# Index read and weight loads in one run on GpSimd, flag read last, contiguous w1 columns, and a new order of the work in an attention + mixture-of-experts kernel

## Chip, cores and metric

One NeuronCore of one Trainium2 chip. The metric is the device time of one execution in microseconds (us). All operands are float32. TensorE is called PE in the rows (PEld is its weight load), VectorE DVE, ScalarE ACT, GpSimd POOL, SyncE SP.

## What is computed

Two attention blocks with 32 inducing points, then a mixture of experts with one expert for each row. Cut to what matters:

```python
B, N, m, C = 4, 11456, 32, 128           # x: [B, N, C]; inducing: [m, C]; E, F = 8, 1024
def mab(q, kv):
    s = scale * (q @ kv.T); s = s - s.max(-1)
    a = exp(s); a /= a.sum(-1) + 1e-9
    return a @ kv
h = mab(inducing, x)                      # [B, 32, C]: needs all of x of its batch
x2 = mab(x, h)                            # [B, N, C]
logits = x2 @ w_gate;  e_idx = argmax(logits)        # one expert for a row
gate_w = softmax(logits)[e_idx];  eom = sigmoid(x2 @ w_output_gate)
out = gate_w * eom[e_idx] * (relu(x2 @ w1[e_idx]) @ w2[e_idx])
```

## The kernel before

The fast path guesses that all rows of a batch choose the same expert (that of the mean of h) and that the signs inside the relu are the same for all rows; then the expert's output is a linear map of the attention weights, and its values can be worked out once for the 32 points (`V`, 32 x 128) instead of for each row. `known` proves the guess at the end and leaves a flag for each batch; where a flag is set, a branch ("general") redoes that batch. It isn't taken here.

A batch is 90 tiles of 128 rows in six chunks: chunk 0 with 10 tiles, five with 16 (1 MB each). For every batch the kernel runs these steps (generators; each `yield Step(...)` names the engine, a planned cost, what it waits for and which ring slots it takes or gives back):

- `bring_in(b, k)`: load a chunk of x on SP's DMA queue into one of 5 chunk buffers (ring `c`, L109), transpose its tiles on PE (L226), copy them from PSUM to `xT` on ACT or DVE (L298). Chunk 0 and the first two full chunks of batch 0 come in two pieces.
- `attend_in(b, i)`: for one or two chunks the scores on PE (L254), max on DVE (L259), exp on ACT (L277), transpose on DVE (L281), and p times x on PE (L291), after which the chunk buffers are given back.
- `finish(b)`: merge the groups to h (`hs`, PE L325/L327, DVE L330 to L343).
- `choose(b)`: PE L352 multiplies the mean of h with the gate weights, DVE takes the index of the largest (L355, L358, tile `ix`), GpSimd reads it into a register (`value_load`, L361) and issues the DMAs of that expert's w1 and w2 (512 KB each, L369 and L374).
- `gates(b)`: small operations on GpSimd or DVE (L380 to L396) and two small matmuls (L399, L415) that make the gate matrix `gb`.
- `values(b)`: PE L426 multiplies h with w1 (four column groups of 256), DVE transposes and masks (L429 to L435), PE L444 multiplies with w2, L452 sums over the four groups, and a copy leaves `vb`, that is V(b).
- `weigh(b, k)`: scores of a chunk against h (PE L520), max (DVE L525, L528), exp (ACT L530).
- `attend_out(b, i)`: for two chunks the gate logits (PE L545) and a chain of small operations (`gate`, L610 to L635) that ends in the scale `sm`; then the output matmuls with `vb` (PE L563) and the scaling of four pieces of each chunk (`scaled`: L586 on DVE, L580 on ACT followed by L582 on GpSimd, L589 on ACT), and the stores on SP's queue (L598).

No loop runs over these steps. `interleave` is a planner that runs when the program is built: it keeps a clock for every engine, and takes at each turn the step that can start first, with a key from the table `ORDER` to decide between steps of the same start. The order in which it takes them is the order of the instructions on each engine; each engine works its queue strictly in that order. SP has one queue for the loads of x and the stores of out, so a load behind a store waits for that store's data. Its model has constants: `LAG` (from the end of a step to who waits for it), `COLD` (until 9 us a step on PE counts double), and fillers: matmuls of the identity that keep PE busy (`fill`, L154), put in wherever the plan has PE idle before `WARM`.

```python
LAG = {"T": 0.2, "V": 0.12, "A": 0.14, "G": 0.15, "D": 2.0, "S": 0.1}
...
if e == "T" and free[e] < WARM:
    fill(int((start - free[e]) / FILL), rings["bank"][-1][1])
```

At the end of the program every engine loads the flag from `flags` (L818) and branches (L819). The two DVE instructions that fill `flags` (L816, L817) and the load are written behind the planned part, where the compiler orders them.

Of the kernel before, what the change touches and what calls it, by code (L numbers as in the profile page):

```python
# [20 lines left out]
EPS = 1e-9
CH = 16
G = 4
# [5 lines left out]
        -362.6, -249.4, -297.0, -141.1, -66.2, -225.8, -56.5, -44.3, -26.1, 0.9, -18.1, -291.1,  # L29
        -91.2, -232.5, -91.6, -90.0, -72.7, -148.2, -142.0, -114.3, -68.9, -12.2, -87.6, 12.3,  # L30
    ],
    "attend_in": [
        -232.4, -227.2, -218.8, -345.7, -218.6, -218.3, -212.8, -232.0, -214.5, -164.2, -143.6, -218.7,
        -147.0, 3.8, -105.9, -148.6,
    ],
    "weigh": [
        -375.2, -216.8, 45.8, -90.0, -326.3, 62.3, -92.7, -171.9, -232.0, -150.7, -162.5, -102.5,
        -19.7, -114.3, -267.8, -92.2, -216.8, -284.7, -213.9, 144.4, -279.9, -332.7, -65.4, -332.0,
    ],
    "attend_out": [-109.6, -67.0, 12.7, -37.8, -310.4, 159.8, 2.0, -51.7, 11.5, -47.5, -1.7, -104.8],  # L40
    "finish": [-0.2, -80.8, -47.5, -116.3],
    "choose": [-80.8, -265.7, -279.2, -368.1],
    "gates": [41.2, -16.3, -2.9, -149.0],
    "values": [-71.8, 12.2, -60.8, -217.9],
    "known": [-85.5],
# [15 lines left out]
def body(ctx: ExitStack, tc: tile.TileContext, x, inducing, w_gate, w_out_gate, w1, w2, out):  # L61
# [93 lines left out]

    def interleave(threads):
        free = dict.fromkeys(LAG, 0.0)
        done = {}
# [689 lines left out]
```

## Time and profile before

| what | value |
|---|---|
| time, three runs | 208.21 us median (207.98, 208.21, 209.38) |
| the profiled execution | 209.38 us; its span, first to last instruction, 207.7 us |
| granted TensorE clock, mean | 0.946 |
| DMA | 51.75 MB, 249 GB/s over the span |

Starts and durations in rows are us from the span's start. [...] The profiled execution is the slowest of the three runs, 0.56% over their median.

### The profile page before, as it was taken

To read this page: it belongs to the slowest core of one execution; us is meant where nothing else is said; L and a number is where in the kernel's file an instruction comes from. 1 tells how busy PE (TensorE), PEld (TensorE's weight loads), DVE (VectorE), ACT (ScalarE), POOL (GpSimd) and SP (SyncE) were. 2 spreads that over 40 slices of the span, in tenths; PEclk is the share of its full clock that TensorE was granted. 3 is DMA by queue.
4 is the path that set the end of the run, shared out by engine and by line. 5 is a ranking of instruction groups with operands and counts; after the bars stand their busy time and mean duration, and the time that the engine had idled before them with its cause. 6 is when DMAs were issued, how large, how long until landed. Compare 5 with 4: busy or idle time off the path is not lost.

```text
span 207.7 us, 6550 instructions
## 1 busy us (share of the span) xinstructions
PE 175.7 (85%) x2627; PEld 123.8 (60%) x2628; DVE 138.7 (67%) x408; ACT 116.0 (56%) x299; POOL 48.1 (23%) x98
## 2 busy tenths in 40 slices
PE   6999998799799899997699999839999958895700
PEld 6987675775583675767268684627587523564700
DVE  2033863557569689894278889738968894999920
ACT  2268285453663755757057564904958882697400
POOL 1000000005001054330012612402325480535510
PEclk9999999999999999999699999979999996999665
DMA  5991765596419308999910999943337999479892
GB/s 180 353 400 21 271 249 196 215 360 264 190 21 372 140 3 248 374 383 385 419 66 14 323 386 396 357 155 126 97 107 307 379 338 349 177 228 371 292 345 108
DMA packets 12675, 51.75 MB, mean 249 GB/s; under 512 B 1760, under 2 KB 1792, under 8 KB 10336
## 3 DMA queue, kind: packets, MB, share of 16 engines
q1 hardware_dynamic: 11152, 47.06, 60.2%
q0 software_dynamic: 1152, 4.19, 5.8%
q8 instruction: 22, 0.36, 0.7%
q14 instruction: 13, 0.11, 0.1%
q10 hardware_dynamic: 336, 0.02, 0.1%
HBM read 27.81 MB, written 23.46 MB: 247 GB/s over the span
## 4 chain that ended last, share of the span: by engine, by line
PE 54%; DMA 19%; DVE 13%; issue 5%; POOL 3%; ACT 1%; POOLq 1%; DVEq 0%
PE bank L226 13%; DMA w1t<-in_moe_w_dram 10%; PE bank L291 9%; PE bank L254 8%; PE bank L563 8%; DMA c<-in_x_dram 6%; DVE ob L586 5%; PE bank L545 4%; PE bank L154 3%; DMA w2t<-in_moe_w_dram 3%; PE bank L520 2%; PE bank L426 2%; PE bank L327 1%; PE bank L444 1%; DVE am L525 1%
## 5 line engine op out<-in xcount | busy, mean ns | idle before, releaser
L298 ACT COPY xT<-bank 128x512 f32<-128x512 f32 (+1 forms) x74 | 39.0, 585 | 26.2 <-PE bank L226 26.0
L226 PEld LDWEIGHTS bank<-ident,c 128*128 128x128 f32 x360 | 39.6, 143 | 15.1 <-issue 6.7
L226 PE MATMUL bank<-ident,c 128*128 128x128 f32 x360 | 45.6, 276 | 3.5 <-DMA c<-in_x_dram 3.2
L582 POOL TENSOR_TENSOR ob<-ob,sm 128x512 f32<-128x512 f32 (+1 forms) x24 | 24.6, 1026 | 36.7 <-ACT ob L580 32.2
L563 PEld LDWEIGHTS bank<-vb,pT 32*128 32x128 f32 x720 | 25.8, 200 | 9.5 <-issue 5.2
L563 PE MATMUL bank<-vb,pT 32*128 32x128 f32 x720 | 30.3, 298 | 1.1 <-DVE lt L610 0.6
L586 DVE TENSOR_TENSOR ob<-bank,sm 128x512 f32<-128x512 f32 (+2 forms) x47 | 29.2, 647 | 2.1 <-PE bank L563 1.6
L580 ACT COPY ob<-bank 128x512 f32<-128x512 f32 (+1 forms) x24 | 13.7, 569 | 24.6 <-issue 10.3
L589 ACT ACTIVATE ob<-bank,sm 128x128 f32<-128x128 f32 x91 | 26.1, 394 | 0.0
L254 PE MATMUL bank<-xT,indT 128*32 128x512 f32 (+1 forms) x192 | 25.1, 591 | 0.4 <-DVE nb L271 0.4
L520 PE MATMUL bank<-xT,hc 128*32 128x512 f32 (+1 forms) x192 | 23.6, 598 | 0.1
L291 PE MATMUL bank<-c,p 128*32 128x128 f32 x720 | 22.8, 274 | 0.2 <-DVE p L281 0.2
L530 ACT ACTIVATE pT<-bank,nq 128x512 f32<-128x512 f32 (+1 forms) x24 | 16.1, 681 | 11.1 <-DVE nq L528 7.4
L259 DVE TENSOR_REDUCE cm<-bank 128x1 f32<-128x512 f32 (+1 forms) x24 | 15.4, 647 | 9.7 <-PE bank L254 9.6
L291 PEld LDWEIGHTS bank<-c,p 128*32 128x32 f32 x720 | 19.9, 110 | 3.3 <-issue 1.2
L298 DVE COPY xT<-bank 128x512 f32<-128x512 f32 (+1 forms) x18 | 12.1, 672 | 14.6 <-PE bank L226 14.6
L277 ACT ACTIVATE bank<-bank,nb 128x512 f32<-128x512 f32 (+1 forms) x24 | 15.5, 647 | 2.2 <-DVE nb L271 2.0
L281 DVE STREAM_TRANSPOSE p<-bank 128x512 f32<-128x512 f32 (+1 forms) x24 | 16.0, 668 | 0.9 <-ACT bank L277 0.8
L525 DVE TENSOR_REDUCE am<-bank 128x1 f32<-128x512 f32 (+1 forms) x24 | 15.2, 642 | 0.7 <-PE bank L520 0.5
L615 POOL TENSOR_SCALAR s<-lt 128x32 f32<-128x32 f32 (+1 forms) x12 | 3.8, 321 | 46.2 <-DVE lt L610 29.9
L545 PE MATMUL bank<-pT,gb 128*32 128x256 f32 (+1 forms) x192 | 12.8, 384 | 0.0
L426 PE MATMUL bank<-w1t,hs 128*32 128x256 f32 x32 | 4.5, 639 | 9.5 <-DMA w1t<-in_moe_w_dram 9.5
(121 smaller groups left out, 177.5 us busy)
## 6 DMA issues: line engine op xcount, KB each, us to landing
c<-in_x_dram SPq DMA_DIRECT2D x18, 1024.0 KB, 8.2
out_dram<-ob SPq DMA_DIRECT2D x30, 512.0 KB, 5.1
out_dram<-ob SPq DMA_DIRECT2D x8, 448.0 KB, 4.1
c<-in_x_dram SPq DMA_DIRECT2D x4, 512.0 KB, 11.0
w1t<-in_moe_w_dram POOLq DMA_DIRECT2D x4, 512.0 KB, 6.2
w2t<-in_moe_w_dram POOLq DMA_DIRECT2D x4, 512.0 KB, 7.1
out_dram<-ob SPq DMA_DIRECT2D x8, 256.0 KB, 4.6
c<-in_x_dram SPq DMA_DIRECT2D x3, 640.0 KB, 10.7
```

What stands on the lines that cost most here:

```text
L226: nc.tensor.transpose(t[:, j - a * G, :], xc[:, j, :], ident)
L254: nc.tensor.matmul(sj[r, 0:n, :], indT, xT[:, 0:n, r], start=True, stop=True)
L291: nc.tensor.matmul(h[r, :], p1[:, j, q, :], xc[:, q, :], start=j == 0 and q < G, stop=j == J - 1 and q >= n - G)
L298: (nc.scalar.copy if e == "A" else nc.vector.tensor_copy)(dst, src)
L520: nc.tensor.matmul(s[g * M : (g + 1) * M, :], st["hc", b], xT[:, q0[g] : q0[g] + w, :], start=True, stop=True)
L525: nc.vector.tensor_reduce(am, s, AX.X, ALU.max, apply_absolute_value=True)
L530: nc.scalar.activation(pT[:, base : base + w, :].rearrange("p a t -> p (a t)"), s, AF.Exp, bias=nq)
L545: nc.tensor.matmul(L[r, u, :], lhs, pT[:, 0:S, r], start=True, stop=True)
L563: nc.tensor.matmul(y[g][:, a, :], pT[r, t + a, :], st["vb", b][r, :], start=True, stop=True)
L582: nc.gpsimd.tensor_tensor(out=o, in0=o, in1=scale_by, op=ALU.mult)
L586: nc.vector.tensor_tensor(out=o, in0=y, in1=scale_by, op=ALU.mult)
L589: nc.scalar.activation(o[:, a, :], y[:, a, :], AF.Copy, scale=sv[:, a : a + 1])
```

## The change

- `choose`: one step on GpSimd holds the index read and both weight loads. In the planner the pair costs GpSimd 2.4, then the DMA queues 2.8, and two steps on a new engine "W" (waiting only) stand for the landing of w1 and, 0.8 later, w2.
- `values`: the w1 matmul streams 256 columns that lie next to each other, where before it took every eighth column in turn; the transpose on DVE that follows takes the stride instead, reading PSUM with steps of 8 elements.
- `known` fills `flags`; the load of the flag stands at the end of the planned part, behind all stores.
- The planner: loads of x no longer wait in the plan for the first piece; a DMA step hands on without its lag; chunk 0 is transposed in pieces of 4 tiles; a model of the clock (`hot`) takes the place of `COLD`; 14 fillers are put in before anything (as 11 and 3 with the matmul of `indT` between), and few more. Fillers go from 23 matmuls (46 records: a float32 matmul shows as two, a transpose as one) to 16.
- A new table `ORDER`, and so a new order on all engines.

```diff
 ORDER = {
     "bring_in": [
-        -362.6, -249.4, -297.0, -141.1, -66.2, -225.8, -56.5, -44.3, -26.1, 0.9, -18.1, -291.1,
+        -253.838, -227.102, -220.31, -44.452, -17.707, -18.373, 213.774, 22.09, 45.955, 69.077, 129.352, 19.815,
...
-LAG = {"T": 0.2, "V": 0.12, "A": 0.14, "G": 0.15, "D": 2.0, "S": 0.1}
+LAG = {"T": 0.2, "V": 0.12, "A": 0.14, "G": 0.15, "D": 2.0, "W": 0.0}
-TAIL = {"D": 2.0, "V": 2.0}
+TAIL = {"D": 3.0, "V": 1.8}
-COLD = 9.0
-WARM = 12.0
-FILL = 0.25
+FIRST = 3.5
+WARM = 8.0
+FILL = 0.15
...
     def interleave(threads):
+        fill(14, 7)
         free = dict.fromkeys(LAG, 0.0)
+        free["T"] = FIRST
...
-                start, end = at[e], at[e] + (2 * c if e == "T" and at[e] < COLD else c)
+                start, end = at[e], at[e] + (c if e != "T" or hot(at[e]) else SLOW * c)
...
-            if e == "T" and free[e] < WARM:
-                fill(int((start - free[e]) / FILL), rings["bank"][-1][1])
+            if e == "T" and FIRST < free[e] < WARM:
+                fill(int((start - free[e]) / FILL), rings["bank"][0][1])
+                hot(free[e], start)
...
+            if e == "D":
+                end = issued
...
     def bring_in(b, k):
-        after = [("h", b - 2)] * (b > 1) + [("x", 0, 0)] * (b + k > 0)
+        after = [("h", b - 2)] * (b > 1)
...
-        na = -(-n // G)
+        na, tt = -(-n // G), 1 if b + k == 0 else TT
...
     def choose(b):
-        yield Step("S", 1.2)
+        yield Step("G", 2.4, take=(("w1", 1),))
         e = ds(nc.gpsimd.value_load(ix[0:1, 0:1], min_val=0, max_val=E - 1), 1)
-        yield Step("D", 1.4, take=(("w1", 1),), post=("w1", b))
         st["w1", b] = load_w1(w1[e])
-        yield Step("D", 1.4, post=("w2", b))
         st["w2", b] = load_w2(w2[e])
+        yield Step("D", 2.8)
+        yield Step("W", 1.4, post=("w1", b))
+        yield Step("W", 0.8, post=("w2", b))
...
     def values(b):
-        zb = bank(slot, [P, NF, M])
+        zb = bank(slot, [P, F // G])
         for g in range(G):
-            cols = w1t[:, g * F // G : (g + 1) * F // G].rearrange("p (t f) -> p f t", f=NF)
+            cols = w1t[:, g * F // G : (g + 1) * F // G]
             nc.tensor.matmul(zb[g * M : (g + 1) * M], hs[:, 0:M], cols, start=True, stop=True)
         z = wp.tile([P, NF, M], F32, name="z")
-        nc.vector.transpose(z, zb)
+        nc.vector.transpose(z, zb.rearrange("p (t f) -> p f t", f=NF))
...
     def known():
+        nc.vector.tensor_copy(flags[:, 0:B], bad[0:1, :])
+        nc.vector.tensor_reduce(flags[:, B : B + 1], bad[0:1, :], AX.X, ALU.max)
...
     with tc.manual_schedule():
         interleave(threads)
+        some = nc.values_load(flags[0:1, B : B + 1], min_val=0, max_val=1)
...
-    nc.vector.tensor_copy(flags[:, 0:B], bad[0:1, :])
-    nc.vector.tensor_reduce(flags[:, B : B + 1], bad[0:1, :], AX.X, ALU.max)
-    some = nc.values_load(flags[0:1, B : B + 1], min_val=0, max_val=1)
```

In the rows of the changed order the same instructions carry other line numbers: L386 is the index read (before L361), L395 and L400 the loads of w1 and w2 (L369, L374), L377 the choosing matmul (L352), L452 the w1 matmul (L426), L549 and L574 those of `weigh` and the gate logits (L520, L545), L592 the output matmul (L563), L425 and L441 the small ones of `gates` (L399, L415), L627 the stores (L598), L676 the load of the flag (L818).

GpSimd's queue, batch 0, from the index read (`TENSOR_LOAD ix`) to the two weight loads; first before, then changed:

```order
L361 TENSOR_LOAD ix
L361 ISA x2
L383 TENSOR_SCALAR q<-ix 128x1
L386 TENSOR_SCALAR one<-rev,q 128x8
L389 TENSOR_TENSOR wq<-wgo,one 128x16
L394 TENSOR_SCALAR wd<-wgo,ws 128x5
L395 TENSOR_SCALAR wd<-wgo,ws 128x3
L396 TENSOR_SCALAR wd<-ws 128x1
L369 ISA
L369 DMA w1t<-in_moe_w_dram 128x1024
L374 ISA
L374 DMA w2t<-in_moe_w_dram 128x1024
```

```order
L386 TENSOR_LOAD ix
L386 ISA x2
L395 ISA
L395 DMA w1t<-in_moe_w_dram 128x1024
L400 ISA
L400 DMA w2t<-in_moe_w_dram 128x1024
```

The six small operations of `gates` that stood between the read and the loads have moved to DVE or behind the loads.

PE's queue, batch 3, from the choosing matmul to the w1 matmul (`w1t,hs`); first before, then changed:

```order
L352 MATMUL bank<-wgo,hs 128x8
L545 MATMUL bank<-pT,gb 32x224 x8
L563 MATMUL bank<-vb,pT 128x128 x16
L520 MATMUL bank<-xT,hc 32x512 x8
L563 MATMUL bank<-vb,pT 128x128 x16
L399 MATMUL bank<-wd,h_2599 128x16
L520 MATMUL bank<-xT,hc 32x384 x4
L426 MATMUL bank<-w1t,hs 32x256 x4
```

```order
L377 MATMUL bank<-wgo,hs 128x8
L549 MATMUL bank<-xT,hc 32x384 x4
L549 MATMUL bank<-xT,hc 32x512 x4
L592 MATMUL bank<-vb,pT 128x128 x16
L549 MATMUL bank<-xT,hc 32x512 x8
L425 MATMUL bank<-wd,h_2616 128x16
L574 MATMUL bank<-pT,gb 32x224 x8
L441 MATMUL bank<-ga,ones 128x32
L592 MATMUL bank<-vb,pT 128x128 x16
L452 MATMUL bank<-w1t,hs 32x256 x4
```

One more group of `weigh` (32x512 x4) and the second small matmul of `gates` stand ahead of the w1 matmul.

SP's queue at the end, the last stores and the load of the flag (`TENSOR_LOAD flags`); first before, then changed:

```order
L598 DMA out_dram<-ob 112x1024
L598 DMA out_dram<-ob 12x1024
L818 TENSOR_LOAD flags
L818 ISA x2
L598 DMA out_dram<-ob 128x1024 x2
L598 DMA out_dram<-ob 128x512 x4
L819 COMPARE_AND_BRANCH
```

```order
L627 DMA out_dram<-ob 112x1024
L627 DMA out_dram<-ob 12x1024
L627 DMA out_dram<-ob 128x1024 x6
L627 DMA out_dram<-ob 128x512 x4
L676 TENSOR_LOAD flags
L676 ISA x2
L845 COMPARE_AND_BRANCH
```

The load of the flag has moved behind the last six stores.

## Rows read from the trace of the kernel before

**Rows 1.** The profile page, part 1: busy us of each engine, share of the span, instructions.

```profile
PE 175.7 (85%) x2627; PEld 123.8 (60%) x2628; DVE 138.7 (67%) x408; ACT 116.0 (56%) x299; POOL 48.1 (23%) x98
```

**Rows 2.** The view of who waited for whom, PE's waits: instruction waited, releaser, us in total, times, longest.

```profile
PE bank L426 <- DMA w1t<-in_moe_w_dram: 9.5, 4, 3.1
...
PE bank L399 <- POOL wd L396: 1.0, 1, 1.0
PE bank L444 <- DMA w2t<-in_moe_w_dram: 0.8, 1, 0.8
```

**Rows 3.** The timeline of PE, the choosing matmul (L352) and the w1 matmul (L426) of batches 0 to 3: start, us, instruction, in brackets the idle time just before it and its releaser.

```profile
46.30 0.36 PE L352 MATMUL bank<-wgo,hs 128*128 128x8 f32 x2 [0.30 <-DVE hs L338]
...
54.40 1.10 PE L426 MATMUL bank<-w1t,hs 128*32 128x256 f32 x8 [1.27 <-DMA w1t<-in_moe_w_dram]
...
86.32 0.39 PE L352 MATMUL bank<-wgo,hs 128*128 128x8 f32 x2
...
100.36 1.13 PE L426 MATMUL bank<-w1t,hs 128*32 128x256 f32 x8 [2.92 <-DMA w1t<-in_moe_w_dram]
...
127.61 0.39 PE L352 MATMUL bank<-wgo,hs 128*128 128x8 f32 x2
...
138.32 1.13 PE L426 MATMUL bank<-w1t,hs 128*32 128x256 f32 x8 [3.15 <-DMA w1t<-in_moe_w_dram]
...
162.55 0.36 PE L352 MATMUL bank<-wgo,hs 128*128 128x8 f32 x2
...
172.16 1.13 PE L426 MATMUL bank<-w1t,hs 128*32 128x256 f32 x8 [2.15 <-DMA w1t<-in_moe_w_dram]
```

**Rows 4.** The chain of work that ended last, its pieces that are weight loads: start, us, what (a DMA's piece runs from issue to landing).

```profile
50.08 4.19 DMA w1t<-in_moe_w_dram
...
90.83 9.40 DMA w1t<-in_moe_w_dram
...
131.64 6.55 DMA w1t<-in_moe_w_dram
...
170.84 7.02 DMA w2t<-in_moe_w_dram
```

**Rows 5.** The timeline of GpSimd: the first operation behind the index read (L383) in batches 0, 2 and 3, and the issue of w1 in batch 3.

```profile
48.11 0.19 POOL L383 TENSOR_SCALAR q<-ix 128x1 f32<-128x1 uint32 x1 [1.83 <-DVE ix L358]
...
130.06 0.19 POOL L383 TENSOR_SCALAR q<-ix 128x1 f32<-128x1 uint32 x1 [0.62 <-DVE am L525]
...
165.01 0.19 POOL L383 TENSOR_SCALAR q<-ix 128x1 f32<-128x1 uint32 x1 [0.66 <-DVE lt L610]
...
166.07 0.61 POOL L369 DMA_DIRECT2D w1t<-in_moe_w_dram  x1
```

**Rows 6.** The table by windows: from:to, length, busy us (instructions) of each engine, granted PE clock, DMA share, GB/s.

```profile
34.50:37.50 3.00, 1.00 (x11) 0.35 (x10) 2.05 (x6) 1.94 (x6) 0.00 (x0) 1.00 0.96 404
54.30:55.60 1.30, 1.20 (x9) 0.35 (x10) 0.03 (x1) 0.24 (x2) 0.00 (x0) 1.00 0.14 57
100.40:103.50 3.10, 3.10 (x24) 1.14 (x28) 1.11 (x3) 0.00 (x0) 0.00 (x0) 0.50 1.01 427
...
138.30:141.00 2.70, 2.68 (x32) 1.62 (x34) 0.90 (x3) 0.00 (x0) 0.00 (x0) 0.50 0.07 27
...
172.20:175.30 3.10, 3.10 (x24) 1.11 (x28) 1.60 (x6) 0.69 (x3) 0.00 (x0) 0.52 0.90 313
150.00:186.00 36.00, 31.53 (x602) 20.59 (x590) 28.70 (x84) 25.57 (x78) 15.39 (x27) 0.95 0.73 269
180.20:198.60 18.40, 13.25 (x232) 9.99 (x230) 17.93 (x47) 12.51 (x38) 8.73 (x13) 0.91 0.83 300
...
193.50:203.70 10.20, 2.74 (x60) 2.55 (x52) 4.77 (x12) 1.17 (x2) 2.10 (x2) 0.67 0.95 349
203.70:207.70 4.00, 0.00 (x0) 0.00 (x0) 0.00 (x0) 0.00 (x0) 0.00 (x0) 0.50 0.09 34
```

**Rows 7.** Groups of instructions, shapes kept apart: count, busy us and mean ns of one, idle before. The w1 matmul, a matmul of the same 256 columns that lie together, the transpose behind the w1 matmul.

```profile
L426 PE MATMUL bank<-w1t,hs 128*32 128x256 f32 x32 | 4.5, 639 | 9.5 <-DMA w1t<-in_moe_w_dram 9.5
...
L545 PE MATMUL bank<-pT,gb 128*32 128x256 f32 x128 | 9.0, 399 | 0.0
...
L429 DVE STREAM_TRANSPOSE z<-bank 128x256 f32<-128x256 f32 x4 | 1.8, 449 | 10.4 <-PE bank L426 10.4
```

**Rows 8.** The timeline of PE at the start: fillers (L154) and the first transposes of x (L226).

```profile
1.60 3.87 PE L154 MATMUL bank<-ident 128*128 128x128 f32 x20 [1.60 <-POOL ident masks.py:199]
...
5.58 2.94 PE L154 MATMUL bank<-ident 128*128 128x128 f32 x24
8.36 2.13 PE L226 MATMUL bank<-ident,c 128*128 128x128 f32 x18
```

**Rows 9.** The chain of work that ended last, pieces around a late load of x and behind V(3) (L452 is its last matmul).

```profile
28.66 1.90 PE bank L226 x16
...
32.49 4.90 DMA c<-in_x_dram
...
180.16 1.85 PE bank L520 x16
182.01 0.76 PE bank L545 x16
```

**Rows 10.** The view of one line: the load of the flag on SP, ns min/median/max.

```profile
L818 SPq TENSOR_LOAD <-flags x1: 1031/1031/1031, 196.0 to 196.0; - x1
```

More of the change, by code (lines that the diff above doesn't have):

```diff
@@ L28 @@
     "bring_in": [
[L29 to L30 removed]
+        -253.838, -227.102, -220.31, -44.452, -17.707, -18.373, 213.774, 22.09, 45.955, 69.077, 129.352, 19.815,
+        -151.252, -150.565, -309.822, -35.387, 2.541, 43.668, 12.74, 209.258, 54.387, -214.157, 227.916, 416.154,
     ],
     "attend_in": [
[L33 to L34 removed]
+        -313.289, -326.078, -210.702, -208.648, 15.407, 30.233, -5.022, -129.073, 61.964, 71.754, 102.009, 72.029,
+        104.26, 284.876, 219.277, 147.818,
     ],
     "weigh": [
[L37 to L45 removed]
+        73.21, 217.755, 369.017, -203.518, 215.252, 1.454, 464.927, 320.253, 277.739, 404.01, 32.48, 204.45,
+        -316.28, 43.47, 34.579, 260.756, 384.698, -292.667, 30.221, 281.833, 67.785, 237.437, 464.917, -233.744,
+    ],
+    "attend_out": [-139.669, 201.185, 177.53, 169.76, 182.472, 316.379, 177.199, 394.483, 130.177, 49.948, 247.511, -212.011],
+    "finish": [319.49, -225.343, 61.493, -245.724],
+    "choose": [-219.482, -247.904, 69.067, 83.802],
+    "gates": [319.572, 90.995, 188.735, 53.281],
+    "values": [19.825, 178.442, 163.927, 55.83],
+    "known": [57.334],
 }
[L48 removed]
+LAG = {"T": 0.2, "V": 0.12, "A": 0.14, "G": 0.15, "D": 2.0, "W": 0.0}
 SWITCH = 0.1
[L50 removed]
+TAIL = {"D": 3.0, "V": 1.8}
 TT = 2
[L52 to L54 removed]
+FIRST = 3.5
+WARM = 8.0
+FILL = 0.15
+WINDOW = 3.413
+IDLE = (0.9, 2.0)
+SLOW = 1.7
 PREFER = 0.4
@@ L154, in fill, with hot @@
                 nc.tensor.matmul(t[:, 0:P], ident, ident, start=True, stop=True)
+    clock = {"window": 1, "busy": 0.0, "hot": True}
+    def hot(at, end=None):
+        w, busy, fast = clock["window"], clock["busy"], clock["hot"]
+        k = int(at / WINDOW)
+        while w < k:
+            w, busy, fast = w + 1, 0.0, WINDOW - busy <= IDLE[fast]
+        if end is not None:
+            while end > (w + 1) * WINDOW:
+                busy += (w + 1) * WINDOW - max(at, w * WINDOW)
+                w, busy, fast = w + 1, 0.0, WINDOW - busy <= IDLE[fast]
+            clock.update(window=w, busy=busy + end - max(at, w * WINDOW), hot=fast)
+        return fast
     def interleave(threads):
+        fill(14, 7)
         free = dict.fromkeys(LAG, 0.0)
+        free["T"] = FIRST
         done = {}
@@ L182, in interleave @@
                 mode = s.mode
+                hot(start, end)
+            issued = end
             end += LAG[e] if end > start else 0.0
@@ L211, in bring_in @@
             yield (bring_rest(b, k, xc, parts[1]),)
-        (tslot,) = yield Step("T", 0.0, take=(("xT", 1),))
+        (tslot,) = yield Step("T", 0.0, [("x", b, k)], take=(("xT", 1),))
         xT = large(tslot, [P, CH, P])
@@ L215, in bring_in @@
         st["xc", b, k] = xc, cslot
-        na = -(-n // G)
-        for a0 in range(0, na, TT):
-            gs = range(a0, min(a0 + TT, na))
-            nj = min(n, (a0 + TT) * G) - a0 * G
+        na, tt = -(-n // G), 1 if b + k == 0 else TT
+        for a0 in range(0, na, tt):
+            gs = range(a0, min(a0 + tt, na))
+            nj = min(n, (a0 + tt) * G) - a0 * G
             after = [("x", b, k, lo) for lo, _ in parts[1:] if lo < a0 * G + nj]
```

7 lines of the change are left out of this document (4 added, 3 removed).

## The prediction

> **What bounds the kernel now.** I read the page's busy shares first. PE is busy 175.7 of 207.7 us, DVE 138.7, nobody else comes near [rows 1], so PE is the engine whose idle time has to be explained. The view of waits gives it: PE waited 9.5 us for w1 in four waits, 1.0 for the gate operations of batch 3 on GpSimd and 0.8 for its w2 [rows 2]. That is 11.3 us. The timeline shows where: the w1 matmul of each batch starts 8.1, 14.0, 10.7 and 9.6 us behind the choosing matmul, and PE stood still for 1.27, 2.92, 3.15 and 2.15 us directly before it [rows 3]. The order of PE's queue has too little work between the two.
>
> [...] And a chain: nothing of batch 3 can be stored before V(3), whose last matmul ends at 180.16 [rows 9], and 5.87 MB of output (11456 rows of 512 B) have to go out after it. So I split the span: 180.16 us up to V(3), and 27.5 behind it. Behind V(3) DVE is busy 17.9 of 18.4 us, and then the DMA engines carry the rest with a share of 0.95 up to 203.7; 4.0 us at the end have next to nothing in them [rows 6].
>
> **Prices.** For work that moves on PE I use one price per shape, from pieces of the chain without waits: 0.118 us for a transpose (16 in 1.90), 0.93 for a group of `weigh` (two in 1.85), 0.76 for a short group of gate logits [rows 9]; output matmuls 0.069, `attend_in` scores 0.92 and 0.056 for each of p times x, in the same way. Summed over the old queue they give 163 us, where the trace has 175.7 less 6.8 of fillers [rows 1, 8] less 2.7 of slow clock (below), 166; so they are 2% low.
>
> **The change, part by part, up to V(3).**
>
> *Start.* In the trace the first transpose comes at 8.36, right behind 44 filler records [rows 8]. Now 28 stand ahead: 3.87 for the first 20, 8 at 2.94/24 = 0.12, and 0.2 for `indT`, so PE is free at 1.60 + 5.0 = 6.6. Has x landed then? A whole 1 MB load took 4.90 us from a freed buffer [rows 9]; the first piece is a quarter of that with nothing ahead of it, and 1.60 + 4.90 = 6.5. I take -1.7. Bounds: 0 (landed just before 8.36) and -1.8.
>
> *w1 columns.* The four w1 matmul groups take 1.10 to 1.13 us each, the same at a granted 0.50 (batches 1 to 3) as at 1.00 (batch 0) [rows 3, 6], so it is not the array that sets their time but how the columns come. A matmul of 256 columns that lie together takes 399 ns where this one takes 639 [rows 7]; eight of them in four column groups would then take 0.5 to 0.7. I take 4 x 0.5 = -2.0, bounds -2.4 and 0. The transpose behind it (449 ns, [rows 7]) now reads PSUM with a stride. No row shows such a read; between no loss and twice its time it costs 0 to 0.45 in each batch, 0 to 1.8 in all, and I take 0, since the other transposes of that kind are priced by elements.
> [...]
>
> *Index read and weight loads in one run.* The six gate operations between the read and the loads go. In batches 0, 2 and 3 the first operation behind the read starts at 48.11, 130.06 and 165.01, w1 of batch 3 is issued at 166.07 [rows 5], w1 of the others at 50.08 and 131.64 [rows 4]; so it can leave 2.0, 1.6 and 1.0 us earlier. For batch 1 I take the smallest, 1.0. w2 of batch 3 left only at 170.84 [rows 4] and now follows at once. What they did on GpSimd now stands on DVE or later, where the small gate matmul has 4 us of PE work ahead of it; if that cover is gone it costs the 1.0 again.
>
> *New order around w1.* PE's work from the choosing matmul to the w1 matmul, by the prices: 6.9, 11.3, 6.4, 6.3 us before; 7.9, 12.8, 8.3, 7.5 now (the rows of batch 3 are in the change). Needed, from the distances above less the earlier issue: 8.1 - 2.0 = 6.1; 14.0 - 1.0 = 13.0; 10.7 - 1.6 = 9.1; 9.6 - 1.0 = 8.6, and for batch 3 1.2 more, because DVE's queue has a transpose and a scaling between h(3) and the index that weren't there. Waits left: 0, 0.2, 0.8, 2.3, with 0.8 for loads that meet other traffic 4.1. Against 11.3: -7.2. Bounds: -11.3, and with every w1 load at the longest landing seen, 9.40 [rows 4], waits of 3.3, 0.1, 3.6 and 5.7, 12.7 in all, that is +1.4.
>
> *Slow clock.* 3.10 + 2.68 + 3.10 us of PE work lie at 0.50 [rows 6]; less the three w1 matmuls, which don't care, 5.5, of which half, 2.7, is loss. One such stretch (batch 3) I leave in: -1.8. Bounds -2.7 and 0.
>
> *Work that moves ahead of V(3).* Two groups of `weigh` and a short one of gate logits stood behind V(3) (1.85 + 0.76, [rows 9]) and now stand before it: +2.6. The w2 matmul and the sum over groups now follow each other, so a copy lies bare between: +0.6 (a guess from 0 to 1, copies of this size being shorter than the 449 ns of [rows 7]).
>
> *Loads of x.* Two chunk buffers come free at once and PE has 2.4 us of work until it needs the first; with 4.90 to landing [rows 9] that is a wait of 2.5. The old order had the same: PE busy 1.00 of 3.00 us at 34.5 to 37.5 [rows 6]. 0, bounds -2 and +3 (the last rival).
>
> *DVE.* Between the w1 matmuls of batches 2 and 3 PE has 34.1 us of work by the prices, and DVE 40.2 by its means; these means count overlaps twice (157.5 for the whole old queue, 138.7 busy, [rows 1]), so 35.4. DVE becomes level with PE there: +2.0, bounds 0 and +10.
>
> Sum up to V(3): -1.7 - 2.0 - 7.2 - 1.8 + 2.6 + 0.6 + 2.0 = -7.5.
>
> **Behind V(3).** DVE loses two groups of `weigh` and one gate chain to the time before, some 4 of its 17.9 us (2 x 0.84 and 2.3 by DVE's means), and is then no longer last. What is: 2.6 us to the first store (10 output matmuls 0.7, the copy, two scalings), 5.87 MB at the 349 GB/s of the last stretch, 16.8, and the 4.0 at the end [rows 6]: 23.4 against 27.5, -4.1. Bounds: -6.4 (at the 404 GB/s of [rows 6]) and 0. The load of the flag held SP for 1.03 us ahead of six stores [rows 10]; behind them it lies beside the landing of the last one. I take 0 for it, from -1 (the stores leave sooner) to +1.2 (it becomes the end).
>
> **The sum.** 207.7 - 7.5 - 4.1 = 196.1; the profiled execution was 1.7 over its span: 197.8; the median of the three runs stands 0.56% below that execution: 196.7 us. That is 11.5 less than 208.21.
>
> **Rivals.**
> *DVE becomes the bound.* For: behind V(3) it is full, and in the last third the two engines are level. From 150 to 186 it was busy 28.70 of 36 us [rows 6], 80%, though it had work; at 80% its 35.4 take 44, ten more than PE's. Against: part of that idle time was PE's waits for w1, which go. +8 on the forecast: 204.7, still faster.
> *The waits stay.* The earlier issue meets more loads of x, and w1 lands as late as the longest seen: +1.4 in place of -7.2, clock and tail unchanged, DVE hidden beside the waits: -1.7 - 2.0 + 1.4 + 2.6 + 0.6 = +0.9, a median of 209.1. For: 4.19 to 9.40 for the same 512 KB [rows 4], which the order can't set. Against: even then batches 0 and 1 wait little.
> *Loads of x behind stores.* In SP's new queue the last load of batch 2 and all six of batch 3 stand behind stores of earlier batches, each of which waits for a scaling on DVE, ACT or GpSimd. If the scalings run late, x comes late, PE has nothing to transpose, h(b) and w1 move back with it. It decides from the point where a store's data is later than 4.90 before PE reaches that chunk; each such load then costs up to 4.90 [rows 9] and a slow stretch of 0.9. Three: +17.4, 214.1, slower. For: the queue is strict, and PE comes to these chunks sooner than it did. Against: the old queue had nine such loads, and by the prices the seven have 3 us or more to spare.
>
> **How the numbers follow.** A measurement here tells about 1% from no change (206.1 to 210.3 is "same"). Forecast, some 190.5 to 202: 0.64. DVE the bound, 202 to 206: 0.18. The waits stay: 0.09. x behind stores, slower: 0.09. Faster 0.82, same 0.09, slower 0.09. For 8 in 10 the range takes the forecast and most of the DVE case: below, all waits and slow stretches gone, 190.5; above 205.5.
>
> **What would show it.** Right: first transposes near 6.6; w1 matmul groups near 0.6; the index read followed by w1's issue within 0.3; PE's waits for w1 in sum under 5; a granted clock of 0.50 in at most one stretch before V(3); V(3) near 173; some 23 us behind it, DMA at a share above 0.9. Wrong: w1 waits above 8, or waits for x above 5 in the second half, or DVE idle below 5% from batch 2 on with PE waiting for it; then the step on the order has failed, not the one on the columns.

## The result, and the profile after

The changed kernel took 200.44 us, median of 4 runs (lowest 198.02), beside 208.8 us for the kernel before: a ratio of 0.951 (0.937 to 0.965). Run again among the experiments it took 198.79 us (median of 6), a ratio of 0.956 (0.949 to 0.963). Predicted were 196.7 us, a ratio of 0.945. So it is faster, inside the range of 190.5 to 205.5, and 2 to 3 us short of the forecast gain of 11.5: the medians give 8.4 and 9.7. Some executions of every kernel take over one per cent longer than its others; the ratios here leave these out (so 0.951 is less than 200.44 divided by 208.8), and where a profiled execution is one of them, its time stands with its rows.

Its first profiled execution took 201.15 us, more than two of its other three runs; the rows here are from one of 198.18 us (span 196.6), among the runs of the second time, unless the text says otherwise. First part 1 of the page, against [rows 1]:

```profile
PE 171.3 (87%) x2613; PEld 119.6 (61%) x2614; DVE 137.6 (70%) x416; ACT 115.9 (59%) x296; POOL 44.4 (23%) x87
```

PE lost 4.4 us of busy time, DVE 1.1. The larger loss is in PE's idle time: 6.7 of the 11.1 us by which the span is shorter. PE's waits, against [rows 2]:

```profile
PE bank L452 <- DMA w1t<-in_moe_w_dram: 3.6, 2, 1.9
PE bank L251 <- DMA c<-in_x_dram: 2.3, 3, 1.6
...
PE bank L316 <- DVE p L306: 1.2, 1, 1.2
PE bank L574 <- DVE se L662: 0.9, 1, 0.9
PE bank L293 <- DVE cg L287: 0.7, 1, 0.7
PE bank L592 <- DVE ob L615: 0.5, 1, 0.5
PE bank L425 <- POOL wd L422: 0.4, 1, 0.4
PE bank L478 <- ACT va L323: 0.4, 1, 0.4
PE bank L592 <- ACT vb L323: 0.4, 1, 0.4
```

For w1, w2 and the gate operations together PE waits 4.0 us where it waited 11.3. The timeline of PE, choosing matmul (L377), w1 matmul (L452) and V(3)'s last matmul (L478), against [rows 3]:

```profile
44.67 0.29 PE L377 MATMUL bank<-wgo,hs 128*128 128x8 f32 x2
...
52.36 0.61 PE L452 MATMUL bank<-w1t,hs 128*32 128x256 f32 x8
...
71.96 0.29 PE L377 MATMUL bank<-wgo,hs 128*128 128x8 f32 x2
...
84.95 0.61 PE L452 MATMUL bank<-w1t,hs 128*32 128x256 f32 x8
...
117.87 0.39 PE L377 MATMUL bank<-wgo,hs 128*128 128x8 f32 x2
...
128.75 0.64 PE L452 MATMUL bank<-w1t,hs 128*32 128x256 f32 x8 [1.67 <-DMA w1t<-in_moe_w_dram]
...
156.30 0.39 PE L377 MATMUL bank<-wgo,hs 128*128 128x8 f32 x2
...
166.86 0.64 PE L452 MATMUL bank<-w1t,hs 128*32 128x256 f32 x8 [1.93 <-DMA w1t<-in_moe_w_dram]
...
172.21 0.49 PE L478 MATMUL bank<-va,same_m 128*128 128x128 f32 x2 [0.39 <-ACT va L323]
```

Batches 0 and 1 no longer wait, and V(3) ends at 172.7 instead of 180.2. The windows directly behind the two waits left, and from V(3) to the end, against [rows 6]:

```profile
129.20:132.00 2.80, 2.80 (x52) 1.42 (x44) 2.55 (x8) 0.41 (x1) 0.55 (x2) 1.00 1.04 433
167.50:170.10 2.60, 2.60 (x56) 1.62 (x60) 2.55 (x6) 1.40 (x5) 0.93 (x2) 1.00 1.03 418
...
184.00:190.00 6.00, 2.24 (x34) 1.93 (x33) 3.54 (x9) 0.59 (x1) 1.13 (x2) 0.50 1.02 413
...
172.70:196.60 23.90, 10.48 (x200) 8.47 (x200) 14.19 (x38) 9.13 (x27) 7.74 (x11) 0.70 0.75 282
```

(From:to, length, busy us of PE, PEld, DVE, ACT and POOL, granted PE clock as a share of full speed, DMA share, GB/s.) The clock stays at 1.00 behind both waits. Behind V(3) the time is 23.9 us where it was 27.5; PE has 10.48 us of work left there (13.25 before), DVE 14.19 (17.93 before). Now the groups of the w1 matmul and the transpose behind it, against [rows 7], and PE's first transposes of x, against [rows 8]:

```profile
L452 PE MATMUL bank<-w1t,hs 128*32 128x256 f32 x32 | 2.5, 383 | 3.6 <-DMA w1t<-in_moe_w_dram 3.6
...
L455 DVE STREAM_TRANSPOSE z<-bank 128x256 f32<-128x256 f32 x4 | 1.8, 445 | 3.5 <-PE bank L452 3.5
```

```profile
6.78 0.60 PE L251 MATMUL bank<-ident,c 128*128 128x128 f32 x4
```

Last, where w1 leaves, against [rows 5]: when DVE has the index (L383) and when GpSimd issues w1 (L395), in batches 2 and 3.

```profile
119.41 0.16 DVE L383 FIND_INDEX8 ix<-m,bank 128x8 uint32<-128x8 f32 x1
...
121.55 0.65 POOL L395 DMA_DIRECT2D w1t<-in_moe_w_dram  x1 [2.84 <-DVE ws L418]
...
157.34 0.16 DVE L383 FIND_INDEX8 ix<-m,bank 128x8 uint32<-128x8 f32 x1
...
158.94 0.63 POOL L395 DMA_DIRECT2D w1t<-in_moe_w_dram  x1 [0.35 <-issue]
```

From the end of the index to the issue it is 1.98 and 1.44 us, though nothing but the read stands between the two in the queue any more (in batch 3 a 1.05 us scaling and the first gate operation end 0.35 us before the issue); in batches 0 and 1 it is 1.60 and 1.28. The read itself (L386), ns min/median/max over the four batches:

```profile
L386 POOLq TENSOR_LOAD <-ix x4: 307/449/934, 45.5 to 157.5; - x4
```

It starts 0.04 us behind the index and takes 497, 307, 934 and 401 ns in batches 0 to 3 (before: 508, 1267, 497 and 721). The rest, about 1.0 us in every batch, is instructions on registers, of the read and of the load, and from the last of them to the DMA's own record 0.53 to 0.62 us.

From the choosing matmul's start to the issue it is 3.68 us in batch 2, where it was 4.03, and 2.64 in batch 3, where it was 3.52. Batches 0 and 1 gained more: 2.38 for 3.78, and 2.54 for 4.51. When w1 lands shows in the chain of work that ended last, against [rows 4]:

```profile
121.55 7.06 DMA w1t<-in_moe_w_dram
...
158.94 7.74 DMA w1t<-in_moe_w_dram
```

In batches 2 and 3 that is 10.7 and 10.4 us behind the start of the choosing matmul. Before it was 10.6 and 9.5, as the loads took only 6.55 and 6.0 us. So there w1 left sooner and landed no sooner. In batches 0 and 1 it landed 6.6 and 7.7 us behind the choosing matmul, where it was 8.0 and 13.9.

### The profile page after: what moved, and what is told of

It reads as the page before. It is cut to its first block, busy times and chain, and to the rows that moved or that the text cites. A ratio compares the mean times of both kernels' runs of the same rounds, so it can differ in the third digit from the quotient of the medians.

```text
span 199.5 us, 6515 instructions
## 1 busy us (share of the span) xinstructions
PE 174.6 (88%) x2613; PEld 120.8 (61%) x2614; DVE 137.7 (69%) x416; ACT 116.2 (58%) x296; POOL 44.4 (22%) x87
## 5 line engine op out<-in xcount | busy, mean ns | idle before, releaser
L323 ACT COPY xT<-bank 128x512 f32<-128x512 f32 (+1 forms) x76 | 40.2, 580 | 17.8 <-PE bank L251 17.4
L251 PE MATMUL bank<-ident,c 128*128 128x128 f32 x360 | 47.0, 277 | 0.9 <-DMA c<-in_x_dram 0.6
L615 DVE TENSOR_TENSOR ob<-bank,sm 128x512 f32<-128x512 f32 (+1 forms) x48 | 30.2, 654 | 2.6 <-PE bank L592 2.4
L592 PE MATMUL bank<-vb,pT 32*128 32x128 f32 x720 | 29.8, 294 | 1.4 <-DVE ob L615 0.5
L592 PEld LDWEIGHTS bank<-vb,pT 32*128 32x128 f32 x720 | 24.7, 194 | 9.5 <-issue 3.6
L549 PE MATMUL bank<-xT,hc 128*32 128x512 f32 (+1 forms) x192 | 24.5, 602 | 0.2 <-ACT ob L609 0.2
L279 PE MATMUL bank<-xT,indT 128*32 128x512 f32 (+1 forms) x192 | 24.5, 599 | 0.0
L618 ACT ACTIVATE ob<-bank,sm 128x128 f32<-128x128 f32 x84 | 24.1, 394 | 0.0
L554 DVE TENSOR_REDUCE am<-bank 128x1 f32<-128x512 f32 (+1 forms) x24 | 15.7, 655 | 3.3 <-PE bank L549 3.3
L323 DVE COPY xT<-bank 128x512 f32<-128x512 f32 x16 | 11.0, 688 | 8.3 <-PE bank L251 8.2
L574 PE MATMUL bank<-pT,gb 128*32 128x256 f32 (+1 forms) x192 | 12.6, 381 | 1.2 <-DVE se L662 0.9
L406 POOL COPY h<-hs 128x128 f32<-128x128 f32 x4 | 1.2, 289 | 41.2 <-DVE hs L360 41.2
```

The lines of the kernel that those rows point to most:

```text
L251: nc.tensor.transpose(t[:, j - a * G, :], xc[:, j, :], ident)
L279: nc.tensor.matmul(sj[r, 0:n, :], indT, xT[:, 0:n, r], start=True, stop=True)
L323: (nc.scalar.copy if e == "A" else nc.vector.tensor_copy)(dst, src)
L549: nc.tensor.matmul(s[g * M : (g + 1) * M, :], st["hc", b], xT[:, q0[g] : q0[g] + w, :], start=True, stop=True)
L554: nc.vector.tensor_reduce(am, s, AX.X, ALU.max, apply_absolute_value=True)
L592: nc.tensor.matmul(y[g][:, a, :], pT[r, t + a, :], st["vb", b][r, :], start=True, stop=True)
```

## The experiments

Each ratio is against runs of the kernel before on the same chip, with its 95% interval.

### The four small parts, one at a time, in the old order

**Columns.**

```diff
-            cols = w1t[:, g * F // G : (g + 1) * F // G].rearrange("p (t f) -> p f t", f=NF)
+            cols = w1t[:, g * F // G : (g + 1) * F // G]
...
-        nc.vector.transpose(z, zb)
+        nc.vector.transpose(z, zb.rearrange("p (t f) -> p f t", f=NF))
```

> The kernel before with contiguous w1 columns alone; order, loads and flag as before. The prediction priced this edit at -2.0 us (four groups of w1 matmuls from 1.1 to 0.6 us each): 206.2. A second theory comes from the trace of the changed kernel, where contiguous groups took 0.62 us at a granted clock of 1.00 and 1.08 at 0.50, so that the array sets their time there: in the kernel before three of the four groups stand in a slow stretch behind a wait, so only batch 0 gains, about 0.5 us: 207.7, w1 groups 0.6 in batch 0 and 1.1 in batches 1 to 3. A third: the transpose that now reads PSUM with a stride takes up to twice its 449 ns, +1.8: 208 to 210.

Measured: 1.0075 (1.004 to 1.011), no gain and a slight loss. The w1 matmuls in the timeline of this kernel:

```profile
54.87 0.64 PE L426 MATMUL bank<-w1t,hs 128*32 128x256 f32 x8 [1.11 <-DMA w1t<-in_moe_w_dram]
...
99.14 0.64 PE L426 MATMUL bank<-w1t,hs 128*32 128x256 f32 x8 [1.49 <-DMA w1t<-in_moe_w_dram]
...
136.29 1.08 PE L426 MATMUL bank<-w1t,hs 128*32 128x256 f32 x8 [3.42 <-DMA w1t<-in_moe_w_dram]
...
172.26 0.64 PE L426 MATMUL bank<-w1t,hs 128*32 128x256 f32 x8 [2.40 <-DMA w1t<-in_moe_w_dram]
```

Three groups of four shrank from 1.1 to 0.64, and V(3) starts its last matmul only 0.4 us sooner (179.24 for 179.67): PE's wait for w2 grew from 0.8 to 1.7 us. The saved time went into the next wait. The transpose takes 450 ns, so the third theory falls. Of the second, what it says of the clock is right, as the one group behind which the clock is at 0.50, in batch 2, takes 1.08; but it had three such groups. Why the kernel is even 0.75% slower isn't shown. One candidate is the clock: the mean granted clock over all its executions is 0.941, where the kernel before has 0.951 on the same chip. A mean lower by 0.01 is some 4 us of the 207 at a granted 0.50 in place of 1.00, an estimate from these means of up to 2 us for PE. The kernel with fewer fillers below has 0.941 too, the one with all four parts 0.937, while the changed kernel has 0.954.

**Both weight loads right behind the index read.**

```diff
-        yield Step("D", 1.4, take=(("w1", 1),), post=("w1", b))
         st["w1", b] = load_w1(w1[e])
-        yield Step("D", 1.4, post=("w2", b))
         st["w2", b] = load_w2(w2[e])
+        yield Step("D", 1.4, take=(("w1", 1),), post=("w1", b))
+        yield Step("D", 1.4, post=("w2", b))
```

> The kernel before with both weight loads issued right behind the index read, ahead of the small gate operations on GpSimd; PE's and DVE's order stays the old one. Theory of the prediction: w1 leaves 1.0 to 2.0 us earlier in each batch and the PE waits fall by the same, from 11.3 to about 6 us (0, 1.9, 1.5, 1.1 before w1, w2 nothing), and one or two of the three slow stretches go: 202 to 203.5. Rival: when the load starts does not set when it lands, other loads of x do (4.2 to 9.4 us for the same 512 KB): PE waits for w1 stay at 8 to 10 us, time 206.5 to 208.5. A further cost could be the gate operations, now behind two DMA issues: the wait for them at the small gate matmul grows from 1.0 by up to 2.

Measured: 0.992 (0.987 to 0.996), 1.7 us of the 5 expected. In its profiled execution (of 211.4 us) PE waits 4.5 us for w1 (9.5 before), as the theory has it, but 5.0 for x (3.2 before), 1.7 for a DVE operation of the first attention and 1.2 for scalings on DVE. It is also busy for 179.0 us instead of 175.7, at a mean clock of 0.938 (0.946).

**Fewer fillers.**

```diff
+                n = min(int((start - free[e]) / FILL), 16 - filled[0])
+                filled[0] += n
-                fill(int((start - free[e]) / FILL), rings["bank"][-1][1])
+                fill(n, rings["bank"][-1][1])
```

> The kernel before with 7 fewer filler matmuls at the start, nothing else. Theory: PE's first transposes stand behind fillers alone, so they start 1 to 1.4 us earlier than 8.36 and the whole program with them: 206.8 to 207.3. Rival: the start is covered, because x of the next chunks or the copies behind the first transposes come no sooner, or because the first matmuls then run at the slow clock for longer: first transposes earlier, but the first scores at 12.0 as before, and 208.2.

Measured: 1.003 (0.998 to 1.008), the rival. PE comes to x 0.4 us sooner (7.93 for 8.36) and waits for it; its first scores start at 12.93, before at 12.01 (timeline of PE at the start, of an execution of 211.2 us):

```profile
7.93 1.04 PE L229 MATMUL bank<-ident,c 128*128 128x128 f32 x8
9.21 1.31 PE L229 MATMUL bank<-ident,c 128*128 128x128 f32 x10 [0.24 <-DMA c<-in_x_dram]
11.90 1.09 PE L229 MATMUL bank<-ident,c 128*128 128x128 f32 x8 [1.39 <-DMA c<-in_x_dram]
```

**Flag last** (the load moved behind the planned part, the two operations that fill it into `known`).

> The kernel before with the flag loaded behind all stores, and nothing else. The prediction took 0 for it, from -1.0 (stores leave 1.03 us sooner because SP does not stand still for the load) to +1.2 (the load becomes the end). Theory: nothing beyond 0.5 us, 207.7 to 208.7, as the DMA engines are full behind V(3) and hold the stores back in any case. Rival: -1.0, 207.2.

Measured: 1.0016 (0.998 to 1.005). Nothing, as expected.

### The two halves of the change: parts without the order, order without the parts

The first kernel has all four edits above, in the old order and under the old planner.

> The kernel before, in its old order, with the four small parts at once: contiguous w1 columns, both weight loads right behind the index read, 7 fewer fillers, flag loaded last. It tells what the new order adds. By the prediction's terms (start -1.7, columns -2.0, waits by the earlier issue alone -4.6, slow clock -0.9) it would be 199, the order's share then about -2. By the runs of the parts one at a time (+0.75%, -0.84%, +0.3%, +0.2%) they nearly cancel: 207 to 209, and the new order with its planner carries the whole gain of 8 to 10 us. In between, if the columns pay only once the wait behind them is gone: 205 to 206.

Measured: 0.997 (0.990 to 1.003), from four of its twelve executions; the median of all twelve is 209.93, beside 208.52 for the kernel before. Either way no gain is shown. Its PE waits (the profiled execution took 210.2 us):

```profile
PE bank L230 <- DMA c<-in_x_dram: 5.7, 5, 2.5
PE bank L430 <- DMA w1t<-in_moe_w_dram: 4.8, 3, 2.2
...
PE bank L272 <- DVE cg L266: 1.7, 1, 1.7
...
PE bank L569 <- DVE ob L592: 1.6, 2, 1.2
```

The waits for w1 are halved, and in this execution the time has gone to x and to DVE, and into 177.3 us of busy PE at a mean clock of 0.937 (175.7 at 0.946 before). My reading, argued and not shown by a run of its own: an order that was written for late weights has nothing for PE to do when they come early. The second kernel is the changed one with three parts undone (the flag stays behind the stores; one operation on GpSimd stands in for the six gate operations, which stay where the new order has them):

```diff
-        fill(14, 7)
+        fill(22, 7)
...
+        late, wide = sp.tile([P, 6, P], F32, name="late"), ones.unsqueeze(1).broadcast_to([P, 6, P])
+        nc.gpsimd.tensor_tensor(out=late, in0=wide, in1=wide, op=ALU.mult)
         st["w1", b] = load_w1(w1[e])
...
-            cols = w1t[:, g * F // G : (g + 1) * F // G]
+            cols = w1t[:, g * F // G : (g + 1) * F // G].rearrange("p (t f) -> p f t", f=NF)
```

> The new order alone: the changed kernel with strided w1 columns, 8 more fillers, and one operation of some 1.5 us (128x768) on GpSimd between the index read and the weight loads of each batch, as long as the gate operations that stood there; the flag load stays behind the stores. It is the counterpart of the old order with the four parts (0.997 of the kernel before). If parts and order add up, the order alone must give all of the 4 to 5%: 0.955 to 0.965, 199 to 201. If the parts pay only in the new order, as their undoing one at a time says (columns 0.9%, fillers 1%, loads 1.7% for 2.1 us, so some 1.2% for 1.5), the order alone gives 0.98 to 0.99: 204 to 206, and the change is the two together.

Measured: 0.981 (0.975 to 0.987), 204.47 us, the second theory. Of 4.4%, the order alone brings 2.0, the parts alone 0.3, and 2.1 (give or take 1.1, from the three intervals) come only where both are. The 2.1 is an upper figure: the operation that stands in also delays the gate operations behind the loads, and PE waits 2.8 us for them in the profiled execution (of 206.12 us), where the changed kernel has 0.4. The old order didn't have that wait, so the order alone may be worth more than 2.0.

### The parts undone one at a time in the new order

Columns: the changed kernel with the two lines of the first diff turned back.

> The changed kernel with the old strided w1 columns, order the same. By the prediction's term it is 2.0 us slower than the changed kernel (four groups, 0.5 each). By the trace of the changed kernel two of its four groups run at a granted 0.50, where they take 1.08 us as they did with strided columns, so 1.0 slower, w1 groups 1.1 in all four batches. By the run of the columns alone in the old order: no difference, since what stands behind w1's matmul waits for something else.

Measured: 0.965 (0.958 to 0.971), 200.09 beside 198.79 us, 1.3 us; V(3)'s last matmul starts 1.75 us later (173.96 for 172.21). Its groups, shapes kept apart:

```profile
L452 PE MATMUL bank<-w1t,hs 128*32 128x256 f32 x32 | 4.4, 632 | 3.8 <-ACT ex L655 2.2 <-DMA w1t<-in_moe_w_dram 1.6
L455 DVE STREAM_TRANSPOSE z<-bank 128x256 f32<-128x256 f32 x4 | 1.8, 450 | 5.1 <-PE bank L452 5.1
```

The term's 2.0 us are there in PE's time (4.4 for 2.5) and nearly all of it reaches V(3). In the end time the two intervals overlap, but both kernels ran on the same chip, and there five of six runs of the changed kernel lie between 197.5 and 199.5 us and the six of this one between 199.3 and 201.7. The second theory's premise doesn't hold: in the profile of 201.15 us one group of four, not two, took 1.08 us.

Fillers: `fill(14, 7)` made `fill(22, 7)`.

> The changed kernel with 8 more filler matmuls at the start (16 records, 1.0 to 1.9 us), in the new order; nothing else. The prediction's step 'start' gave 1.7 us for the fewer fillers. Theory: in the new order PE has few waits up to batch 2, so what is lost at the start is lost at the end: first transposes near 8.4, 1.0 to 1.4 above the changed kernel, 200. Rival, as in the old order where 7 fewer gave nothing: the time is taken back in the first waits for x, 0.

Measured: 0.9655 (0.960 to 0.971), 1% or 2 us above the changed kernel, again with intervals that overlap. First transposes at 8.92 instead of 6.78; choosing matmuls of batches 0 and 2 at 46.08 and 119.92 (44.67 and 117.87; in the changed kernel's execution of 201.15 us 43.31 and 116.76). So the loss isn't taken back on the way; how large it is the rows don't say, as two executions of one kernel are 1.4 us apart at batch 0.

Weight loads 2.1 us later:

```diff
+        for _ in range(2):
+            nc.gpsimd.tensor_tensor(out=late, in0=wide, in1=wide, op=ALU.mult)
         st["w1", b] = load_w1(w1[e])
```

> The changed kernel with two more operations on GpSimd, 2.1 us in all (128x512, like its scaling of 1.03), between the index read and the first weight load of each batch; every other row of every engine's order as in the changed kernel. It doses the step 'index read and loads in one run': both weight loads leave 2.1 us later. Theory: the distance from the choosing matmul to w1's landing grows by 2.1 in each batch; batches 0 and 1 had cover, 2 and 3 had none, so PE's waits for w1 go from 3.6 to 8 or more and a slow stretch or two come with them: 4 to 7 us above the changed kernel, 203 to 206. Rival: when the load leaves doesn't set when it lands, or the waits are covered by something that ends as late (in batch 3 a bank that ScalarE frees 0.18 us before w1's matmul starts): 0 to 2 us, 199 to 201.

Measured: 0.972 (0.966 to 0.979), 202.99 us, 1.7% or 3.4 us above the changed kernel: by its time nearer the first theory, but not by what happened. From choosing to w1 matmul it is 12.3 and 12.8 us in batches 2 and 3 (10.9 and 10.6 in the changed kernel). The theory had PE wait 8 us or more for w1. In the profiled execution (of 203.74 us) it doesn't wait for w1 in these batches at all; it waits 3.9 us for gate operations, which stand behind the loads on GpSimd, are late too, and feed a small matmul (L428) ahead of the w1 matmul. PE's waits, and its w1 matmuls (L455 here) in the timeline:

```profile
PE bank L428 <- POOL so L636: 2.2, 1, 2.2
...
PE bank L428 <- POOL wd L425: 1.7, 1, 1.7
```

```profile
131.69 0.64 PE L455 MATMUL bank<-w1t,hs 128*32 128x256 f32 x8
...
172.03 0.64 PE L455 MATMUL bank<-w1t,hs 128*32 128x256 f32 x8
```

w1 lands at 131.5 and 171.0, so the late weights lie behind the late gate operations. This run gives no price for late weights alone; how the 3.4 us divide stays open.

### What still bounds it

Constant experts (`e = ds((1, 6, 2, 4)[b], 1)` in place of the value read from the index):

> The changed kernel with the experts' numbers written in as constants, so that the weight loads don't wait for the choosing matmul, the index on VectorE and its read on GpSimd (it leaves the read of the index out). The wait of each load is then for the slot of its tile alone. Theory: PE is the bound up to V(3) and the two waits left (2.6 and 2.0 us) cost themselves and a slow stretch each (0.9): w1 waits 0, no slow stretch before V(3), V(3) 4 to 6 us earlier: 194 to 196. Rival, VectorE as the bound of the last third: the waits for w1 turn into waits for VectorE, 0 to -1.5: 198 to 200.

Measured: 0.953 (0.947 to 0.959), 197.87 us, 0.9 below the changed kernel, with intervals that overlap: the theory's 194 to 196 falls. w1's issue and matmul in batches 2 and 3:

```profile
119.20 0.65 POOL L395 DMA_DIRECT2D w1t<-in_moe_w_dram  x1
...
157.65 0.63 POOL L395 DMA_DIRECT2D w1t<-in_moe_w_dram  x1
```

```profile
127.50 0.64 PE L452 MATMUL bank<-w1t,hs 128*32 128x256 f32 x8 [0.40 <-DMA w1t<-in_moe_w_dram]
...
165.82 0.64 PE L452 MATMUL bank<-w1t,hs 128*32 128x256 f32 x8 [1.90 <-ACT ob L618]
```

Without the index, batch 2 waits 0.40 (1.67 with it): w1 leaves 0.8 us behind the choosing matmul instead of 3.7, but takes 8.2 us instead of 7.1. In batch 3 the load leaves 2.35 us behind the choosing matmul (at 155.30) where it left 2.64: in GpSimd's queue a scaling of 1.05 us and a gate operation stand ahead of it, which end at 157.58. So the run didn't take away what it should in batch 3. The name ScalarE on that wait misleads: w1 lands 8.0 us behind its issue, at 165.65, and the matmul starts at 165.82.

Less work on DVE, batches 2 and 3 (`s[:, 0:P] if b > 1 else s` in the reduction of L554):

> The changed kernel with less work on VectorE: in batches 2 and 3 the largest score of a group of the second attention is taken over a quarter of its columns, 128 of 512 (so the offset of the exponentials is a smaller number than the largest score; the rest of the arithmetic is as before). That takes some 5.3 us from VectorE's 137.6, all in the last third: twelve operations of 676 or 552 ns fall to about 200. The order stays. If VectorE is the bound there (the prediction's rival): 4 to 5 us faster, 194 to 195. If PE and its waits are: up to 1, 198 to 199. In between: what VectorE has queued between the w1 and the w2 matmul of batch 3 (4.3 us, two of these operations among it) is on the path to V(3), that would give 1 to 2.

Measured: 0.961 (0.954 to 0.968) beside 0.956, no gain, though DVE is busy 134.2 us for 137.6 (the twelve operations fell to 279 ns, not 200; 3.4 us in all, not 5.3). A gain of that size is outside the interval: DVE is not the bound of the last third.

The changed kernel again:

> The changed kernel once more beside the others, to have its time on the same chip and over more runs: 198 to 201, 4 to 5% below the kernel before.

Measured: 0.956 (0.949 to 0.963), 198.79 us; the profile is the one above.

## Why the prediction was right, and where it wasn't

The span of 196.6 us stands beside the sum's 196.1. Up to V(3) it is -7.5, as summed; behind it -3.6, where -4.1 was predicted. That is closer than the prediction was: this execution is a short one, and the one of the kernel before the slowest of its three. In the execution of 201.15 us V(3) ends at 175.5, -4.7, and the time behind it is 24.0. By the medians the gain is 8.4 and 9.7 of 11.5. By its steps:

**Start, -1.7.** First transposes at 6.78 where 6.6 was read from the rows. Right in the new order, where 8 more fillers cost some 2 us; in the old one fewer fillers gave nothing, and in the execution shown the pieces of x behind the first weren't there.

**Columns, -2.0.** Right in size (4.5 us of PE time to 2.5). What the reason left out: strided columns took 1.10 us at a granted 1.00 and 1.13 at 0.50 to 0.52 [rows 3, 6], but contiguous ones followed the clock, 0.61 to 0.64 at 1.00 and 1.08 at 0.50, so the gain was some 0.5 us a group at 1.00 and 0.05 at 0.50. The strided read of PSUM was priced at nothing, and cost nothing: the transpose took 445 ns for 449.

**Index read and loads, 1.0 to 2.0 us sooner.** The step that failed. "Followed by w1's issue within 0.3" did not come: 1.3 to 2.0 us. I had let w1 leave where the first operation behind the read started; but some 0.6 us (0.53 to 0.62) between the read and the issue are the load's own and don't go with the six operations, and in batch 2 the read took 0.44 us longer than before. From choosing matmul to issue, batches 0 to 3 gained 1.4, 2.0, 0.35 and 0.9 us instead of 2.0, 1.0, 1.6 and 1.0. And in batches 2 and 3 the earlier issue brought no earlier landing: the loads took 7.1 and 7.7 us instead of 6.55 and 6.0. In that much the rival *the waits stay* was right. PE's waits fell there because PE had more to do between the two matmuls.

**Waits, 11.3 to 4.1.** Measured 4.0. By batch 0, 0, 1.67 and 1.93 before w1; predicted were 0, 0.2, 0.8, 2.3 and 0.8 for traffic. The order gave PE the work it needed; that the total fits so closely is luck, since the issue in batch 2 was over a microsecond later than thought, and w1 landed 10.7 and 10.4 us behind the choosing matmuls of batches 2 and 3 where 9.1 and 9.8 were reckoned, before the 0.8 for traffic.

**Slow clock, -1.8, one stretch left.** In the kernel before, the granted clock was 0.50 to 0.52 for some 3 us behind the waits of 2.92, 3.15 and 2.15 us, and 1.00 behind that of 1.27 [rows 3, 6]. Now there is none before V(3) in the execution of 198.18 us: the granted clock is 1.00 in every window up to 180. In the one of 201.15 there were two; its w1 matmuls and the windows behind them:

```profile
128.31 1.08 PE L452 MATMUL bank<-w1t,hs 128*32 128x256 f32 x8 [2.59 <-DMA w1t<-in_moe_w_dram]
...
168.11 0.64 PE L452 MATMUL bank<-w1t,hs 128*32 128x256 f32 x8 [1.97 <-DMA w1t<-in_moe_w_dram]
```

```profile
128.90:131.90 3.00, 3.00 (x24) 0.71 (x15) 2.37 (x7) 0.41 (x1) 0.55 (x2) 0.53 0.92 384
168.70:171.70 3.00, 3.00 (x43) 1.71 (x44) 2.24 (x5) 1.31 (x5) 0.86 (x2) 0.59 1.02 418
```

V(3) comes 2.8 us later there, though the choosing matmul of batch 2 came 1.1 us sooner. Of the 3.9 us lost between, 2.3 go in batch 2 (0.9 of longer wait, the rest at the lower clock behind it, a mean of 0.53) and 1.6 in batch 3 (all but 0.04 of it at the lower clock, a mean of 0.59). The term is real, and it is a part of the kernel's scatter.

**Moved work +2.6, bare copies +0.6, x 0, DVE +2.0.** PE's work behind V(3) fell by 2.8; the copies are waited for 0.4 + 0.4; waits for x fell from 3.2 to 2.3. PE's longer waits for DVE sum to 3.3 us (1.2, 0.9, 0.7, 0.5), but the two of 1.2 and 0.7 stand at 28 to 30 us, in the first attention, not in the last third, and the 0.5 behind V(3). The 0.9 of batch 3 stands ahead of the wait for w1, which would be longer without it. So the +2.0 was priced in the wrong place, and the run with less work on DVE shows that the rival built on that stretch (204.7 us) had no ground. That the sum up to V(3) fits to 0.1 us is luck: it held 2.0 for DVE in the last third, which wasn't paid there, and a slow stretch (0.9) that didn't come, and nothing for the 1.9 us of waits for DVE in the first attention.

**Behind V(3), -4.1.** DVE lost 3.7 us there, as priced, and from 184 to 190 the DMA engines are the bound, with a share of 1.02 and 413 GB/s. Over the whole stretch the share is 0.75, where the forecast had above 0.9.

What the sum left unsaid is a condition. It added start, columns and waits with the new order in place, and there undoing one of them costs about its price (columns 1.3 us, fillers 2.0, each with intervals that overlap). But they can't be had without it: alone they give 0.3% together, the order alone 2.0% or more, all of it 4.4%.

## What to carry to other kernels

Where the order of a queue is fixed, a part that got faster saved time here only if the order had work to put in its place (the parts 0.3% without the new order, both together 4.4%); otherwise the saving reappeared as the next wait (w1 to x, columns to w2, fillers to x) or, it seems, as time at the lower clock. So price such a part and the new order together, and run both halves apart: the change without the order and the order without the change. When instructions are removed between a register read and the DMA that uses it, first take off what the read and the DMA's own issue need (here 0.3 to 0.9 and some 0.6 us), and count the gain at the landing, not at the issue.

## What the runs showed of the hardware that was not expected

- A matmul of 256 columns took 632 to 639 ns (means) when its moving columns lay 32 bytes apart, and about the same at either clock (in the kernel before, medians of 632 at a granted 1.00 and 639 to 644 at 0.50 to 0.52); 379 to 383 ns when they lay together at 1.00, and 607 to 634 at 0.50.
- The length of a wait alone didn't tell whether the clock fell behind it. Behind 1.67 and 1.93 us it stayed at 1.00, also behind 2.40 (columns in the old order); behind 1.97, 2.15 and 2.59 its mean over the next 3 us was 0.52 to 0.59.
- Between the index on DVE and the DMA that GpSimd issues with it lay 1.3 to 2.0 us: the read into the register took 0.31 to 0.93 us (up to 1.27 in the kernel before), the instructions on registers and the DMA's own issue about 1.0. MAX8 and FIND_INDEX8 have another DVE operation of 0.67 us between them in batch 2; putting the two next to each other was not tried.
- The same load of 512 KB took 4.2 to 7.7 us from issue to landing in one execution; it took longest in batches 2 and 3, where it left sooner than before.
